# A kernel of Fourier mixing and a gated feed-forward layer on one core: the order of the first loads

## The chip, the core and the metric

The kernel runs on one core of one Trainium2 chip. The metric is device time in microseconds (us) of one execution; the lower the better. TensorE does the matrix products, VectorE and ScalarE prepare their operands and take the results out, GpSimd does a little arithmetic and issues some transfers, SyncE issues most loads.

## What is computed

The reference, cut to what matters (one batch, sequence S = 2048, width D = 640, hidden F = 1536):

```python
x = A_x
xn = _layernorm(x, axis=-1)
a = einsum("bsd,ed->bse", xn, dft_hid_re)
b = einsum("bsd,ed->bse", xn, dft_hid_im)
s = einsum("ts,bse->bte", dft_seq_re, a) - einsum("ts,bse->bte", dft_seq_im, b)
g = silu((silu(xn @ w_gate) * (xn @ w_up)) @ w_down)
return x + s * g
```

The rows of x are normalised; the sequence transform (2048 x 2048, a real and an imaginary matrix) and the hidden transform (640 x 640) are applied; a gated feed-forward layer works on the same normalised rows; the two results are multiplied and added to x.

## The kernel before

All is in float32. To get its precision from products with one pass, each operand is split into a high half (the rounded value, a copy on ScalarE) and a low half (the rest, a subtraction on VectorE), and every product is done as three matmuls: high by high, high by low, low by high (`split`, `mm3`). The large products follow a Strassen scheme, so that sums of blocks are operands too.

The work comes in stages: the sequence transform in four passes (`seq(0)` to `seq(3)`), the hidden transform (`hid_s`), then gate and up and down for two halves of the sequence (`gate_up`, `down`). All operations are first recorded in a plan with a due time, `Plan.schedule` gives each a planned start, `Plan.place` gives the buffers their places in on-chip memory from those times, and then all are written out in the order of their planned starts. Each engine runs its own instructions in that order. In the first pass (k == 0) the planned starts are fixed by hand (`pl.fixed`). The trace names the helper at line 82 (`Engine.__getattr__`, through which every operation goes) for all of them, so instructions are told apart by their tiles.

The opening of the first pass is written in `opening()`, with tables of times in us: OPEN_DMA is the order of the first loads, OPEN_LN the times of the layer norm of the row tiles, OPEN_T those of the splits of the row tiles, OPEN_S those of the splits of the sequence matrices. A row tile is 128 rows of x with all 640 columns (320 KB, tile xn, from in_x). An operand is 128 x 1024 elements of the real or imaginary sequence matrix (512 KB, tile raw, from in_cs); it serves two row tiles, 512 columns each. In OPEN_DMA an entry (k,) is row tile k, and an entry (i, g) is the operand of pair g, real for i = 0 and imaginary for i = 1. The loop over OPEN_DMA gives the entries planned starts 0.45 us apart, and SyncE issues them in that order.

The products of the opening go over row tiles kk = 0 to 7, and for each tile first the real and then the imaginary operand (in tile 7 the other way round). Each has three products with 512 columns: two into a pair of banks and one into a third bank. Those of tile 0 are done unsplit in float32, two weight loads each; those of the others are the three matmuls of `mm3`, so nine weight loads for each operand. Tile 0 is normalised in an own, shorter way. For the others VectorE takes the statistics (bn_stats, bn_aggr), ScalarE the root, VectorE the reciprocals, ScalarE normalises the tile in place and copies its high half, VectorE makes the low half. Eleven matmuls on a tile of zeros (`busy`) run on TensorE before the first product.

```python
t = -6.0
for what in OPEN_DMA:
    if len(what) == 1:
        load_x(what[0], at(t), nc.sync)
    else:
        fetch(what[0], what[1], t, *what[2:])
    t += 0.45
```

Of the kernel before, what the change touches and what calls it, by code (L numbers as in the profile page):

```python
# [278 lines left out]
def tile_fnet_swiglu(  # L279
# [448 lines left out]


    OPEN_DMA = ((0,), (0, 0), (1,), (1, 0), (2,), (3,), (0, 1), (1, 1), (4,), (5,), (0, 2), (1, 2), (6,), (7,), (0, 3), (1, 3))  # L730
    OPEN_LN = ((0, 1, (-2.5,), (-1.4, -1.0, -0.5), (0.4,)),
               (1, 1, (0.5,), (1.6, 1.9), (2.8,)),
               (2, 1, (3.5,), (5.0, 5.3), (6.1,)),
# [8 lines left out]
    def seq(k):  # L742
# [112 lines left out]
        def opening():  # L855
# [566 lines left out]
```

## Time and profile before

| what | value |
|---|---|
| median of 3 runs | 969.66 us (969.62 to 969.9) |
| the profiled execution, its own time | 969.83 us |
| its span, first to last instruction | 967.6 us |
| TensorE busy | 961.7 us, 99% of the span |
| VectorE busy | 734.6 us, 76% |
| ScalarE busy | 488.6 us, 50% |
| GpSimd busy | 121.3 us, 13% |
| mean granted clock of TensorE | 0.999 |

The profile is of one execution, by the hardware profiler. PE is TensorE's matmuls, PEld its weight loads (which overlap the matmuls), DVE is VectorE, ACT ScalarE, POOL GpSimd, SP SyncE; a q behind the name is the engine's sequencer, which issues transfers. A row of the timeline has start, length, engine, line, operation, output<-inputs, shapes, count, and in brackets the idle time of the engine ahead of it with what ended it. A tile is named without its number: hl is a split operand, raw an unsplit one, xn the row tiles, sm, mv, bst and rowst the small results of the layer norm, ps the banks of the products. KB are 1024 bytes in the DMA views; MB and GB/s are decimal.

### The profile page before, as it was taken

What the parts mean: (1) busy time and instruction counts of PE and PEld (TensorE: products, weight loads), DVE (VectorE), ACT (ScalarE), POOL (GpSimd) and SP (SyncE); (2) the same over time, 40 slices, a digit from 0 to 9 for tenths busy, and PEclk for the clock granted to TensorE, in tenths of its full rate; (3) what the DMA queues carried; (4) which work ended last, traced back from release to release, by engine and by line L of the source; (5) the groups of instructions that cost most, each with busy time, mean ns of one, the idle gap of its engine ahead of it and who ended that gap; (6) DMA issues with size and microseconds to landing.
All of it is one profiled execution on the core that took longest, in us unless ns stands there. A gap on an engine that the chain in (4) does not pass through costs nothing.

```text
span 967.6 us, 11521 instructions
## 1 busy us (share of the span) xinstructions
PE 961.7 (99%) x4235; PEld 792.0 (82%) x4235; DVE 734.6 (76%) x932; ACT 488.6 (50%) x676; POOL 121.3 (13%) x184
## 2 busy tenths in 40 slices
PE   9999999999999999999999999999999999999998
PEld 5888888888888888888888888888888888888887
DVE  7889668757774687676987898999978666666775
ACT  5686445454545455544356555563446444444341
POOL 1460211011101110111100211210002000000000
PEclk9999999999999999999999999999999999999999
DMA  9997848494938497778673374439699330105793
GB/s 352 283 249 215 233 147 229 152 271 106 231 109 255 109 236 263 208 196 253 170 213 131 141 265 155 168 136 289 222 292 256 99 133 4 55 1 163 240 346 131
DMA packets 64056, 186.50 MB, mean 193 GB/s; under 512 B 6528, under 2 KB 10368, under 8 KB 64000
## 3 DMA queue, kind: packets, MB, share of 16 engines
q1 hardware_dynamic: 45952, 125.45, 39.0%
q0 software_dynamic: 18048, 60.32, 24.2%
q8 instruction: 33, 0.54, 0.2%
q14 instruction: 23, 0.19, 0.1%
HBM read 151.39 MB, written 34.36 MB: 192 GB/s over the span
## 4 chain that ended last, share of the span: by engine, by line
PE 99%; DMA 0%; DVE 0%; ACT 0%; issue 0%; DVEq 0%; ACTq 0%
PE ps L82 99%; DMA xn<-in_x 0%; DVE raw L82 0%; DVE bst L82 0%; DVE sm L82 0%; ACT raw L82 0%; ACT sm L82 0%; DVE mv L82 0%; DVEq L82 0%; ACTq L82 0%
## 5 line engine op out<-in xcount | busy, mean ns | idle before, releaser
L82 PE MATMUL ps<-hl 128*128 128x512 f32 (+1 forms) x3258 | 780.1, 388 | 0.0
L82 PEld LDWEIGHTS ps<-hl 128*128 128x128 f32 x3258 | 610.1, 188 | 126.6 <-DVE hl L82 0.6
L82 DVE TENSOR_TENSOR hl<-raw,hl 128x1024 fp32r<-128x1024 f32 (+5 forms) x360 | 346.5, 994 | 134.3 <-ACT hl L82 94.4
L82 ACT ACTIVATE hl<-raw 128x1024 fp32r<-128x1024 f32 (+6 forms) x416 | 325.0, 826 | 170.3 <-DVE raw L82 84.8
L82 PE MATMUL ps<-hl,hl 128*128 128x512 f32 (+1 forms) x954 | 259.9, 388 | 0.0
L82 ACT ACTIVATE raw<-ps 128x512 f32<-128x512 f32 (+1 forms) x144 | 97.9, 681 | 231.4 <-PE ps L82 225.2
L82 PEld LDWEIGHTS ps<-hl,hl 128*128 128x128 f32 x954 | 179.0, 188 | 36.9
L82 DVE TENSOR_TENSOR raw<-raw 128x1024 f32<-128x1024 f32 (+7 forms) x216 | 178.6, 849 | 19.8 <-ACT raw L82 15.5
L82 DVE TENSOR_TENSOR raw<-ps,raw 128x512 f32<-128x512 f32 (+1 forms) x95 | 77.2, 814 | 48.4 <-PE ps L82 47.6
L82 DVE TENSOR_TENSOR raw<-raw,raw 128x512 f32<-128x512 f32 (+3 forms) x50 | 44.2, 892 | 6.5 <-ACT raw L82 4.3
L82 ACT ACTIVATE hl<-xn 128x1024 fp32r<-128x1024 f32 (+3 forms) x61 | 42.2, 723 | 13.6 <-PE ps L82 9.1
L82 POOL DMA_DIRECT2D p_dram<-raw x24 | 16.4, 686 | 251.4 <-DVE raw L82 215.7
L82 ACT ACTIVATE raw<-raw 128x512 f32<-128x512 f32 (+1 forms) x30 | 21.5, 718 | 46.7 <-DVE raw L82 46.7
L82 DVE TENSOR_TENSOR hl<-xn,hl 128x1024 fp32r<-128x1024 f32 (+3 forms) x50 | 40.8, 833 | 4.0 <-PE ps L82 3.9
L82 POOL DMA_DIRECT2D raw<-in_cs x36 | 32.5, 984 | 57.7 <-DMA raw<-in_cs 29.1
L82 DVE SCALAR_TENSOR_TENSOR hl<-raw,hl 128x256 fp32r<-128x256 f32 (+4 forms) x56 | 32.7, 586 | 4.0 <-ACT hl L82 4.0
L82 POOL DMA_DIRECT2D out<-raw x10 | 6.9, 689 | 226.6 <-DVE raw L82 197.3
L82 POOL DMA_DIRECT2D d_p<-hl x28 | 15.2, 543 | 71.4 <-ACT hl L82 59.6
L82 ACT ACTIVATE xn<-xn,sm,rowst 128x640 f32<-128x640 f32 (+1 forms) x16 | 14.1, 906 | 5.3 <-DVE sm L82 3.6
L82 DVE BATCH_NORM_STATS2 bst<-xn 128x6 f32<-128x320 f32 x32 | 13.7, 479 | 4.0 <-DMA xn<-in_x 4.0
L82 POOL DMA_DIRECT2D y_dram<-raw x12 | 8.2, 683 | 64.6 <-DVE raw L82 46.2
L82 POOL DMA_DIRECT2D raw<-p_dram x8 | 10.1, 1267 | 44.7 <-DVE raw L82 26.3
(42 smaller groups left out, 84.3 us busy)
## 6 DMA issues: line engine op xcount, KB each, us to landing
raw<-in_cs SPq DMA_DIRECT2D x84, 512.0 KB, 7.0
hl<-d_p SPq DMA_DIRECT2D x56, 384.0 KB, 5.0
raw<-in_cs POOLq DMA_DIRECT2D x36, 512.0 KB, 9.8
raw<-in_wb SPq DMA_DIRECT2D x24, 640.0 KB, 4.7
d_p<-hl POOLq DMA_DIRECT2D x28, 384.0 KB, 4.0
p_dram<-raw POOLq DMA_DIRECT2D x16, 512.0 KB, 4.4
raw<-p_dram SPq DMA_DIRECT2D x8, 768.0 KB, 8.5
xn<-in_x SPq DMA_DIRECT2D x16, 320.0 KB, 9.8
```

What stands on the lines that cost most here:

```text
L82: return real(*args, **kw)
```

## The change

Two pairs of neighbours in OPEN_DMA change places: the first imaginary operand is loaded ahead of row tile 1, and the second real operand ahead of row tile 3. Nothing else is edited.

```diff
-    OPEN_DMA = ((0,), (0, 0), (1,), (1, 0), (2,), (3,), (0, 1), (1, 1), (4,), (5,), (0, 2), (1, 2), (6,), (7,), (0, 3), (1, 3))
+    OPEN_DMA = ((0,), (0, 0), (1, 0), (1,), (2,), (0, 1), (3,), (1, 1), (4,), (5,), (0, 2), (1, 2), (6,), (7,), (0, 3), (1, 3))
```

## Rows read from the trace of the kernel before

**Rows 1.** The page, part 4: shares of the chain by engine.

```profile
PE 99%; DMA 0%; DVE 0%; ACT 0%; issue 0%; DVEq 0%; ACTq 0%
```

**Rows 2.** The chain in order of time: start, length, what.

```profile
0.73 3.01 DMA xn<-in_x
...
6.46 956.86 PE ps L82 x4224
```

**Rows 3.** Groups of weight loads, 17 to 962.5 us: busy, mean | idle before, releasers.

```profile
L82 PEld LDWEIGHTS ps<-hl 128*128 128x128 f32 x3234 | 605.8, 188 | 124.9
L82 PEld LDWEIGHTS ps<-hl,hl 128*128 128x128 f32 x952 | 178.6, 188 | 36.9
```

**Rows 4.** Timeline of SyncE's queue, 0 to 7 us.

```profile
1.16 0.42 SPq L82 DMA_DIRECT2D raw<-in_cs  x1
1.63 0.42 SPq L82 DMA_DIRECT2D xn<-in_x  x1
2.10 0.43 SPq L82 DMA_DIRECT2D raw<-in_cs  x1
...
6.87 0.33 SPq L82 DMA_DIRECT2D raw<-in_cs  x1
```

**Rows 5.** DMA issues: the ones at 1.16 and 1.63 us, us to landing last.

```profile
raw<-in_cs SPq DMA_DIRECT2D x1, 512.0 KB, 4.1
...
xn<-in_x SPq DMA_DIRECT2D x1, 320.0 KB, 5.2
```

**Rows 6.** Windows between landings: length, engines busy, PEclk, DMA share, GB/s.

```profile
5.24:6.86 1.62, 1.34 (x4) 0.33 (x3) 1.31 (x7) 0.65 (x2) 0.00 (x0) 1.00 1.04 268
6.86:9.21 2.35, 2.35 (x6) 0.76 (x4) 1.82 (x8) 1.11 (x2) 0.19 (x1) 1.00 0.91 304
10.98:12.23 1.25, 1.25 (x5) 0.64 (x4) 1.10 (x6) 0.78 (x3) 0.25 (x1) 1.00 1.01 408
```

**Rows 7.** Timeline of the weight loads, 6.4 to 17 us.

```profile
8.28 0.19 PEld L82 LDWEIGHTS ps<-raw,xn 128*128 128x128 f32 x1 [0.24 <-issue]
9.25 0.30 PEld L82 LDWEIGHTS ps<-raw 128*128 128x128 f32 x2 [0.78 <-DMA raw<-in_cs]
...
11.50 0.19 PEld L82 LDWEIGHTS ps<-hl 128*128 128x128 f32 x1 [0.24 <-issue]
11.93 4.09 PEld L82 LDWEIGHTS ps<-hl 128*128 128x128 f32 x18 [0.24 <-DVE hl L82]
16.42 0.76 PEld L82 LDWEIGHTS ps<-hl 128*128 128x128 f32 x4 [0.40 <-DVE hl L82]
```

**Rows 8.** Timeline of VectorE, 7 to 18.5 us.

```profile
7.09 0.88 DVE L82 BATCH_NORM_STATS2 bst<-xn 128x6 f32<-128x320 f32 x2
...
10.25 0.89 DVE L82 BATCH_NORM_STATS2 bst<-xn 128x6 f32<-128x320 f32 x2 [0.20 <-DMA xn<-in_x]
...
13.20 0.88 DVE L82 BATCH_NORM_STATS2 bst<-xn 128x6 f32<-128x320 f32 x2
...
14.61 0.42 DVE L82 SCALAR_TENSOR_TENSOR hl<-xn,hl 128x256 fp32r<-128x256 f32 x1 [0.28 <-ACT hl L82]
...
15.15 1.22 DVE L82 TENSOR_TENSOR hl<-raw,hl 128x1024 fp32r<-128x1024 f32 x1
```

**Rows 9.** Timeline of ScalarE, 8 to 18 us.

```profile
9.49 0.92 ACT L82 ACTIVATE xn<-xn,sm,rowst 128x640 f32<-128x640 f32 x1 [0.95 <-DVE sm L82]
10.44 0.61 ACT L82 ACTIVATE hl<-xn 128x256 fp32r<-128x256 f32 x2
...
12.25 1.06 ACT L82 ACTIVATE hl<-raw 128x1024 fp32r<-128x1024 f32 x1 [0.49 <-DMA raw<-in_cs]
```

**Rows 10.** Windows at the end, columns as in rows 6.

```profile
963.31:965.00 1.69, 0.00 (x0) 0.00 (x0) 0.85 (x2) 0.38 (x1) 0.00 (x0) 1.00 0.40 155
965.00:966.00 1.00, 0.00 (x0) 0.00 (x0) 0.00 (x0) 0.00 (x0) 0.00 (x0) 0.71 0.37 131
```

## The prediction

> **Names.** x0, x1, x2, x3 are the first row tiles (320 KB each). R0, R1 are the first two real operands and I0, I1 the imaginary ones; each is 512 KB and serves a pair of row tiles (R0 and I0 serve x0 and x1, R1 and I1 serve x2 and x3). Step k is the products of row tile k, first the real three, then the imaginary three. Before: x0 R0 x1 I0 x2 x3 R1 I1. After: x0 R0 I0 x1 x2 R1 x3 I1.
>
> **What bounds the kernel now.** I read the chain that ended last first: 99% of the span is TensorE [rows 1], and in order of time the chain is 3.01 us of waiting for x0, 2.7 us of layer norm, and from 6.46 us on TensorE without a break for 956.86 us [rows 2]. Then the weight loads: from 17 us to the end of the products not one of them waits for another engine [rows 3]. Two things follow. What is lost or gained before 17 us moves the end by the same amount, since no later wait can swallow it. And nothing behind the opening has anything left to give.
>
> In the opening TensorE stops twice after its start [rows 7]. The load at 9.25 us waits for I0. The loads before it came every 0.43 us, so 8.71 was due; a load that starts a pause over is followed by the next after 0.11 us and not 0.43, so the pause costs 9.25 + 0.11 - 9.14 = 0.22 us. The load at 16.42 is the second of step 2. It waits for VectorE, which makes the low half of R1 from 15.15 to 16.37 [rows 8]; by the pace of 0.23 us (18 loads in 4.09 us) it was due at 16.07 and the next at 16.30; the next came 0.11 behind it, at 16.53, so this pause costs 0.23 us.
>
> Who sets 16.37? VectorE. From 7.09 on it runs in its written order: statistics of x1, its root, low half of R0, statistics of x2, low halves of x1, and so on, with a few tenths idle [rows 8]. x1 landed at 6.83 (issued at 1.63, 5.2 us later [rows 4, 5]; SyncE's issue at 6.87 is released by it) and VectorE took it 0.26 us later, at once after x0's work. So row tile 1 has almost no slack now.
>
> **The change, part by part.** No engine's instruction is added or removed: four entries of the list OPEN_DMA change places in pairs, each with a planned start 0.45 us away from the old one. All operations of the first real pass carry fixed planned times, so VectorE, ScalarE, GpSimd and TensorE keep their order, and only SyncE's order changes. The 0.42 us that an issue takes, row tile or operand [rows 4], is the same in any order.
>
> *I0 earlier.* It is put ahead of 320 KB that took 1.62 us between two landings [rows 6] but 0.8 to 1.1 us by its bytes at the 408 and 304 GB/s of the stretches behind (328 thousand bytes each; I take 0.9). It lands at some 9.21 - 0.9 = 8.3 us, before 8.71. The pause of 0.22 us at step 0's imaginary half goes; step 1 could then start at 11.71 instead of 11.93.
>
> *x1 later.* The transfers of one queue land in the order of issue, so x1 now lands when the bytes of x0, R0, x1 and I0 are all there. That is the moment at which I0 landed before: 9.21 us (the release of the load at 9.25 [rows 7]). So x1 moves from 6.83 to 9.21, and its statistics from 7.09 to 9.23: +2.14 us. Bounds: if I0 moved at the 1.25 us that R1 took between its neighbour's landing and its own [rows 6], x1 would land at 6.83 + 1.25 = 8.08 (+1.01). If x1 still had some 0.4 us to go on the slowest engine behind I0, it would land at 9.6 (+2.5). I take 9.21, since it is the same bytes in the same early stretch, which ran at 268 and 304 GB/s and not at 408 [rows 6].
>
> The Trainium skill (DMA: Bandwidth & Descriptors, section Specifications) gives a ceiling of 435 GB/s for the core's DMA engines, by which I0 would delay x1 by an estimated 1.21 us; the later stretch at 408 GB/s agrees, the early one does not. By that page the sum below would be 970.3 us.
>
> *From x1's delay to TensorE.* Behind x1 VectorE runs its chain with the same lengths, +2.14. The 0.20 us that it now idles for x2 at 10.25 are used up, but this helps only the low halves of x1: the root of x2 comes from ScalarE, whose work on x1 is 2.14 late as well. ScalarE waits 0.49 us for R1 at 12.25 [rows 9]. After the change R1 is there by then (below), so ScalarE is late by about 1.65 from there. VectorE idles 0.28 us for ScalarE at 14.61 [rows 8]; counted from the earliest start that the 0.09 us overlap of neighbouring rows allows (14.24) this is 0.37 us, and it is swallowed. So the low half of x2 moves by 2.14 - 0.37 = 1.77 (to 16.38), and the low half of R1 ends at 18.14 instead of 16.37.
>
> TensorE: step 1 needs x1's high half. It now ends at 11.05 (9.49 + 0.92 for the normalised rows, then 0.61 for two copies [rows 9]); the first and larger copy, which is all that the load needs, ends some 0.2 us sooner, at 10.86, and will at 13.0. So step 1 starts at 13.15 instead of 11.71: 1.44 us idle. Its third load, due at 13.40, needs the low half, which ends at 13.54: 0.18 more, of which 0.05 are left after the restart. Eighteen products at 0.23 bring step 2 to 17.4; its second load comes at 18.18 instead of 16.42. **TensorE is 1.76 us later there.** As a ledger: idle 1.44 + 0.05 + 0.03 + 0.67 = 2.19 new, less 0.22 + 0.23 of today's pauses, gives 1.74; the two agree. Behind it VectorE is late by 1.77 and TensorE by 1.76, so their distance is today's, and today it is enough at every load [rows 3].
>
> *R1 ahead of x3.* R1 would land about 0.8 us earlier (12.23 to 11.4), x3 at R1's old 12.23. x3 is first used at 13.20 [rows 8], 15.3 after the change: nothing waits for it. R1's use at 12.25 is moved to 13.8 by x1: its earlier landing is worth nothing beyond the 0.49 us above. Alone, without x1's delay, this half would free the 0.23 us pause at 16.42. So this part counts for 0 here, and 0.23 us gain if x1 were in time.
>
> *The queue.* SyncE's ninth and later issues each wait for the landing of the one eight before, as 6.87 shows [rows 4]. The eleventh will wait for I0 (8.3 instead of 6.87) and the twelfth for x1 (9.2, as now for I0). Six transfers are in flight in front of them then, so their data is late by nothing.
>
> **Sum.** The profiled execution took 969.83 us, of which 967.6 are the span; +1.76 gives a span of 969.4 and 971.6. The median of the three runs is 969.66, 0.17 below it, so against the median: 969.66 + 1.76 = **971.4 us**, +0.18%. A change of 0.2% is 1.94 us, about what a measurement of this kernel can tell from no change; the forecast stands just inside it.
>
> **Rivals.**
> 1. *I0 is quick in its new place.* The early stretch is slow for another reason than I0's bytes, and x1 comes only 1.25 to 1.8 us later (lands 8.1 to 8.65). Then the delay is the landing less 7.44: 0.64 to 1.2 us, 970.3 to 970.9. For it: R0, of the same size, landed at 5.26 (issued 1.16, 4.1 later [rows 4, 5]), 1.5 us behind x0 at 3.74 [rows 2]. Against it: x1 itself moved at only 268 GB/s in 5.24 to 6.86 [rows 6].
> 2. *The pause lowers TensorE's clock.* TensorE stands still for 1.44 us from 11.7 on, longer than anywhere between its first and last product now. If the granted clock falls from 2.4 to 1.2 GHz behind it, the 18 products of step 1 take up to 8.2 instead of 4.1 us [rows 7]; step 2's second load then comes as late as 21.4 instead of 18.18, and with part of that the total is +3 to +5 us: 973 to 974.6. For it: at the tail the last product ends at 963.3, and the granted clock is still 1.00 until 965 and 0.71 in the next microsecond [rows 10]: it does fall soon after a stop. Against it: that stop is longer, and full speed held through the shorter pauses. The Trainium skill (TensorE: Matmul & The Clock Gate, Part 1) says that the throttled state is the default and activity releases it; the fall at the tail agrees, and no row here shows a pause of this length.
> 3. *Not slower.* Both landings overlap on the 16 DMA engines so far that x1 lands by 7.44. Up to there the slack at 14.61 swallows its delay and the time stays at 969.7; with x1 quite in time both pauses, 0.22 and 0.23, would go: 969.2 us. It decides at 7.44 us, 0.6 behind today's landing. Against it: the 524 thousand bytes of I0 in 0.6 us would be 870 GB/s, and the fastest stretch of [rows 6] has 408.
> 4. *The change does not do only what it says.* The planned starts of I0 and R1 move by 0.45 us, and these enter the placement of buffers; another placement would bring other waits anywhere, a few tenths to 3 us either way. Against it: the order in which these buffers come up stays the same, and their neighbours in time too.
>
> **How the numbers follow.** Forecast (x1 between 8.65 and 9.6, +1.2 to +2.2): 0.70, with about a quarter of it above +1.94. Rival 1: 0.15. Rival 2: 0.10. Rival 3: 0.02. Rival 4: 0.03. The range takes the forecast's own, 970.9 to 971.9, and most of rival 1, and reaches a little over the upper bound: 970.3 to 972.2. Slower by over 0.2%: 0.18 + 0.10 + 0.02 = 0.30; faster: 0.02; within: 0.68.
>
> **What the profile after would show.** x1's statistics start at about 9.23; the loads of step 0's imaginary half run on at 8.71 without a wait; the first load of step 1 comes near 13.05 released by ScalarE; the second of step 2 near 18.2 released by VectorE; no wait behind 19 us; granted clock 1.00 throughout. A statistics start under 8.7 means rival 1; a granted clock under 1.00 between 11 and 20 us means rival 2. A wait of weight loads after 20 us would make the sum wrong.

## The result, and the profile after

| what | before | after |
|---|---|---|
| median (14 runs each) | 969.78 us | 971.52 us |
| lowest to highest | 969.54 to 969.96 | 971.14 to 972.70 |
| the profiled execution, its own time | 969.83 us | 971.50 us |
| its span | 967.6 us | 969.3 us |

The change makes the kernel slower: by 1.74 us or 0.18% between the medians, with a ratio of 1.0020 and a 95% interval of 1.0013 to 1.0028. Forecast were 971.4 us (+0.18%) within 970.3 to 972.2. The median sits just inside the bound of 0.2%, as forecast, and the ratio on it.

The first view is the chain that ended last, in order of time (start, length, what). Before, it began with the transfer of x0 [rows 2]:

```profile
2.11 7.00 DMA xn<-in_x
...
9.13 0.90 DVE bst L82 x2
...
11.54 0.93 ACT xn L82
```

It now begins with the transfer of x1, issued at 2.11 us and landed at 9.11, and goes through the statistics, the root and the normalising of row tile 1. x0 is no longer on it. The timeline of VectorE shows the same wait and what follows from it:

```profile
9.13 0.89 DVE L82 BATCH_NORM_STATS2 bst<-xn 128x6 f32<-128x320 f32 x2 [2.24 <-DMA xn<-in_x]
...
12.02 0.88 DVE L82 BATCH_NORM_STATS2 bst<-xn 128x6 f32<-128x320 f32 x2
...
16.30 0.37 DVE L82 SCALAR_TENSOR_TENSOR hl<-xn,hl 128x256 fp32r<-128x256 f32 x1
...
16.79 1.22 DVE L82 TENSOR_TENSOR hl<-raw,hl 128x1024 fp32r<-128x1024 f32 x1
```

VectorE stands still for 2.24 us until x1 is there; its statistics start 2.04 us later than in [rows 8] (7.09). The wait for x2 and the idle 0.28 us ahead of the low half of x2, both in [rows 8], are used up, and the low half of R1 starts at 16.79 instead of 15.15: of 2.04 us, 1.64 arrive there.

The weight loads of TensorE (to be held against [rows 7]):

```profile
8.68 0.19 PEld L82 LDWEIGHTS ps<-raw 128*128 128x128 f32 x1 [0.24 <-issue]
...
10.82 0.19 PEld L82 LDWEIGHTS ps<-raw,xn 128*128 128x128 f32 x1 [0.24 <-issue]
12.96 0.30 PEld L82 LDWEIGHTS ps<-hl 128*128 128x128 f32 x2 [1.95 <-ACT hl L82]
13.49 1.68 PEld L82 LDWEIGHTS ps<-hl 128*128 128x128 f32 x8 [0.23 <-DVE hl L82]
15.39 1.90 PEld L82 LDWEIGHTS ps<-hl 128*128 128x128 f32 x9 [0.22 <-DVE hl L82]
18.06 0.77 PEld L82 LDWEIGHTS ps<-hl 128*128 128x128 f32 x4 [0.77 <-DVE hl L82]
```

The gain that the change makes is there: the load at 8.68 (step 0's imaginary half) runs on without the wait for I0 that stood at 9.25. Then TensorE has nothing: the first load of step 1 comes at 12.96, released by ScalarE's high half of x1, and the second of step 2 at 18.06 instead of 16.42. That is 1.64 us, and the span is 1.7 us longer. Behind it no load waits, as before [rows 3]; the groups of weight loads from 19 to 964 us name no releaser here either:

```profile
L82 PEld LDWEIGHTS ps<-hl 128*128 128x128 f32 x3232 | 605.5, 188 | 124.9
L82 PEld LDWEIGHTS ps<-hl,hl 128*128 128x128 f32 x952 | 178.6, 188 | 36.8
```

ScalarE takes R1 without the wait of 0.49 us in [rows 9]:

```profile
13.54 0.28 ACT L82 ACTIVATE sm<-mv,sm 128x1 f32<-128x1 f32 x1
13.72 1.04 ACT L82 ACTIVATE hl<-raw 128x1024 fp32r<-128x1024 f32 x1
```

The clock did not move. Windows of the pause of step 1, of the steps behind it and of the rest (columns as in [rows 6]; PEclk is the third number from the end):

```profile
11.25:13.10 1.85, 0.73 (x3) 0.14 (x2) 1.78 (x7) 1.53 (x4) 0.00 (x0) 1.00 1.02 410
13.10:20.00 6.90, 6.55 (x27) 4.80 (x28) 6.29 (x20) 5.58 (x11) 0.51 (x2) 1.00 1.03 419
20.00:962.00 942.00, 942.00 (x4166) 780.58 (x4165) 719.82 (x888) 476.74 (x656) 119.31 (x172) 1.00 0.63 190
```

### The profile page after: what moved, and what is told of

Same layout as the page of the kernel before. It is cut to its first block, busy times and chain, and to the rows that moved or that the text cites. A ratio compares the mean times of both kernels' runs of the same rounds, so it can differ in the third digit from the quotient of the medians.

```text
span 969.3 us, 11521 instructions
## 1 busy us (share of the span) xinstructions
PE 962.2 (99%) x4235; PEld 792.1 (82%) x4235; DVE 734.4 (76%) x932; ACT 488.3 (50%) x676; POOL 121.0 (12%) x184
## 4 chain that ended last, share of the span: by engine, by line
PE 98%; DMA 1%; DVE 1%; ACT 0%; SPq 0%; issue 0%; DVEq 0%
PE ps L82 98%; DMA xn<-in_x 1%; DVE hl L82 0%; DVE bst L82 0%; SPq L82 0%; DVE sm L82 0%; ACT xn L82 0%; DVE raw L82 0%; ACT hl L82 0%; ACT sm L82 0%; DVE mv L82 0%; ACT raw L82 0%; DVE rowst L82 0%; DVEq L82 0%
## 5 line engine op out<-in xcount | busy, mean ns | idle before, releaser
L82 POOL DMA_DIRECT2D raw<-in_xt x6 | 6.9, 1294 | 70.6 <-DVE raw L82 70.6
```

The lines of the kernel that those rows point to most:

```text
L82: return real(*args, **kw)
```

## The experiments

The theory: the whole loss is the landing of x1, and from 7.44 us on each microsecond of it is one of the time. x0 to x3, R0, R1, I0 and I1 are as in the prediction. A single execution differs from the next by a few tenths of a microsecond, so the profiled execution is read beside its own time, and the medians (11 runs where not said otherwise) stand with their ratio to before.

**Only the first swap (e1_i0_only).**

```diff
-    OPEN_DMA = ((0,), (0, 0), (1,), (1, 0), (2,), (3,), (0, 1), (1, 1), (4,), (5,), (0, 2), (1, 2), (6,), (7,), (0, 3), (1, 3))
+    OPEN_DMA = ((0,), (0, 0), (1, 0), (1,), (2,), (3,), (0, 1), (1, 1), (4,), (5,), (0, 2), (1, 2), (6,), (7,), (0, 3), (1, 3))
```

> Only the first swap: I0 ahead of x1, with x3 ahead of R1 as before. Theory (the whole loss is x1's later landing, carried by VectorE's chain): x1 lands at 9.1 us again, R1 at about 12 and so ahead of ScalarE's use at 13.7; the second load of step 2 comes near 18.1 and the time is that of both swaps, 971.5 us. Rival (the swap of R1 and x3 takes or gives a share of its own): the time differs from 971.5 by 0.2 us or more, and some wait between 12 and 18 us is another one.

Measured: 971.51 us, ratio 1.0019 (1.0010 to 1.0028); before 969.77. The weight loads of its profile:

```profile
12.79 0.30 PEld L82 LDWEIGHTS ps<-hl 128*128 128x128 f32 x2 [1.70 <-ACT hl L82]
...
17.89 0.76 PEld L82 LDWEIGHTS ps<-hl 128*128 128x128 f32 x4 [0.77 <-DVE hl L82]
```

They are those of both swaps, 0.17 us sooner, and x1 landed 0.16 sooner too (8.95). I0 ahead of x1 is the whole loss; the swap of R1 and x3 adds nothing to it and takes nothing off.

**Only the second swap (e2_r1_only, and the same kernel profiled again, e10_r1_again).**

```diff
-    OPEN_DMA = ((0,), (0, 0), (1,), (1, 0), (2,), (3,), (0, 1), (1, 1), (4,), (5,), (0, 2), (1, 2), (6,), (7,), (0, 3), (1, 3))
+    OPEN_DMA = ((0,), (0, 0), (1,), (1, 0), (2,), (0, 1), (3,), (1, 1), (4,), (5,), (0, 2), (1, 2), (6,), (7,), (0, 3), (1, 3))
```

> Only the second swap: R1 ahead of x3, with x1 ahead of I0 as before. Theory: x1 is in time (lands near 6.8), ScalarE no longer waits for R1 at 12.25, the pause of 0.23 us at the second load of step 2 goes and the pause for I0 at step 0 stays: 969.5 us, 0.2 less than before. Rival (x3 is what is late next, or VectorE is held by something else): the pause stays, 969.7 us or more.

> A second look at e2_r1_only, in which I0 landed at 9.78 and not at 9.21 as before, and TensorE waited for it. If R1 right behind I0 delays it as a rule, I0 lands behind 9.5 again and the time is 969.9 or more; if that landing was chance, it is near 9.2, the pauses are 0.2 us and none at step 2, and the time is near 969.5.

Measured: 969.90 us, ratio 1.0001 (0.9992 to 1.0010); the second profile 969.91 in one run. The weight loads of the first profile, then of the second, up to 17.5 us:

```profile
9.82 0.30 PEld L82 LDWEIGHTS ps<-raw 128*128 128x128 f32 x2 [1.68 <-DMA raw<-in_cs]
...
12.51 5.00 PEld L82 LDWEIGHTS ps<-hl 128*128 128x128 f32 x22 [0.24 <-DVE sm L82]
```

```profile
9.60 0.30 PEld L82 LDWEIGHTS ps<-raw 128*128 128x128 f32 x2 [1.09 <-DMA raw<-in_cs]
...
12.28 5.21 PEld L82 LDWEIGHTS ps<-hl 128*128 128x128 f32 x23 [0.24 <-DVE sm L82]
```

The pause at step 2 did go: 22 and 23 loads in a row, across the place where one waited at 16.42. But nothing came of it, since TensorE now waits longer for I0, which landed at 9.78 and 9.56 and not at 9.21. The time is that of the rival, for another reason than the rival's: the pause it wanted to stay is gone. The pause at step 2 had been a reserve. Three profiles have R1 ahead of x3, and x1 ahead of the whole of I0 in the queue. In them I0 landed 0.35 us (e10_r1_again), 0.57 (e2_r1_only) and 0.80 (e7_r1_in_slot, below) later than before, and the products ended only 0.06, 0.29 and 0.53 us later. So before, I0 could have landed some 0.23 us later at no cost, though no run tries that in the old order. That R1 close behind I0 delays it fits both profiles and isn't shown by them.

**Half of I0 ahead of x1 (e3_half_i0).** Its first half serves step 0, its second step 1.

```diff
-    OPEN_DMA = ((0,), (0, 0), (1,), (1, 0), (2,), (3,), (0, 1), (1, 1), (4,), (5,), (0, 2), (1, 2), (6,), (7,), (0, 3), (1, 3))
+    OPEN_DMA = ((0,), (0, 0), (1, 0, 0), (1,), (1, 0, 1), (2,), (0, 1), (3,), (1, 1), (4,), (5,), (0, 2), (1, 2), (6,), (7,), (0, 3), (1, 3))
```

> Both swaps, but I0 is loaded as two halves of 256 KB: the half of row tile 0 ahead of x1, the half of row tile 1 behind it. A dose of half. Theory (loss = landing of x1 less 7.44): x1 lands at 7.5 to 8.0, the loss is 0.1 to 0.6 us, 969.8 to 970.3; no pause for I0 at step 0. Rival (it is the number or order of transfers, or TensorE's pause as such, and not x1's landing): 971 us or more.

Measured: 971.36 us, ratio 1.0016 (1.0007 to 1.0025); the profiled execution took 970.63. By the median the rival holds, by the profile the theory does, for VectorE's and TensorE's timelines show an opening as fast as before:

```profile
7.45 0.89 DVE L82 BATCH_NORM_STATS2 bst<-xn 128x6 f32<-128x320 f32 x2 [0.21 <-DMA xn<-in_x]
...
16.37 1.23 PEld L82 LDWEIGHTS ps<-hl 128*128 128x128 f32 x6 [0.36 <-DVE hl L82]
```

x1 landed at 7.43, and step 2's second load came at 16.37, 0.05 earlier than before. The products ended at 963.26 us against 963.30. Yet the span is 968.4, not 967.6: from the last product to the end it took 5.15 us, before 4.31. The next two kernels take this apart. The profiled execution is the fastest of the 11: the median lies 1.59 us above that of before, and the 0.75 us of it that the end does not explain are in no profile.

**One transfer more, and nothing else (e8_seventeenth).** The last operand of the opening is loaded as two halves.

```diff
-    OPEN_DMA = ((0,), (0, 0), (1,), (1, 0), (2,), (3,), (0, 1), (1, 1), (4,), (5,), (0, 2), (1, 2), (6,), (7,), (0, 3), (1, 3))
+    OPEN_DMA = ((0,), (0, 0), (1,), (1, 0), (2,), (3,), (0, 1), (1, 1), (4,), (5,), (0, 2), (1, 2), (6,), (7,), (0, 3), (1, 3, 0), (1, 3, 1))
```

> The order of before, with the last operand of the opening (imaginary, fourth pair) loaded as two halves, so SyncE issues one transfer more. Theory: the opening is as before and the products end at the same time; at the end SyncE's waits for its eight semaphores stand in a fixed order, the last output now signals the first of them instead of the last, and the seven waits behind it come after the landing: 970.6 us, 0.84 more, all of it behind the last product. Rival (the order of the waits costs nothing): 969.8 us, and the stretch behind the last product stays at 4.31 us.

Measured: 970.69 us, ratio 1.0010 (1.0002 to 1.0019), 0.99 more than before (969.70) and near the 970.6 of the theory. What SyncE waited for at the end of the span, first before, then here:

```profile
SPq L1418 <- DMA out<-raw: 0.7, 1, 0.7
```

```profile
SPq L1418 <- DMA out<-raw: 1.5, 1, 1.5
```

The products ended at 963.17, no later than before, and the rest took 5.13 us instead of 4.31. SyncE's transfers signal eight semaphores (counters that tell of a landing) in turn, and at the end of the program SyncE waits for the eight in a fixed order. Before, the last output signals the last of them, and no other wait for a landing stands behind it. With one transfer more it signals the first: released at 966.49, the seven others follow one by one until 967.32. So 0.82 us belong to the number of transfers, and to nothing in the opening.

The same profile shows what set step 2's second load in the old order:

```profile
16.29 1.23 PEld L82 LDWEIGHTS ps<-hl 128*128 128x128 f32 x6 [0.32 <-DVE hl L82]
```

R1 landed at 12.10 instead of 12.23, and the load came 0.13 us earlier than at 16.42: it follows R1 there.

**Half of I0 ahead of x1, transfers as many as before (e9_half_16).** The order of e3_half_i0, with the entry (7,) left out and row tiles 6 and 7 in one transfer.

```diff
-                if len(what) == 1:
+                if what == (6,):
+                    load_x2(6, at(t), nc.sync)
+                elif len(what) == 1:
...
+    def load_x2(k, lead, eng):
+        pl.prod(lead, lambda: eng.dma_start(
+            xn_tiles(k, 2), x[k * P:(k + 2) * P, :].rearrange("(k p) d -> p k d", p=P)), [], [(xn, k), (xn, k + 1)])
```

> As e3_half_i0 (half of I0 ahead of x1, half behind it, R1 ahead of x3), but row tiles 6 and 7 are one transfer, so that SyncE's transfers are as many as before. Theory: the 0.84 us between the last product and the end of the span that e3_half_i0 had more than before go, and what is left is the landing of x1 less 7.44 (0 to 0.75 us): 969.8 to 970.5 us. Rival (the 0.84 us come from the halves, or from the opening): the time stays within 0.3 us of e3_half_i0, 971.1 or more.

Measured: 970.51 us, ratio 1.0010 (1.0001 to 1.0019), 0.85 less than e3_half_i0, or 0.78 with each against its own before (969.70 here, 969.77 there). It is at the upper end of the theory, and the rival falls: the stretch behind the last product is back at 4.33 us.

```profile
7.88 0.89 DVE L82 BATCH_NORM_STATS2 bst<-xn 128x6 f32<-128x320 f32 x2 [0.71 <-DMA xn<-in_x]
...
16.81 0.77 PEld L82 LDWEIGHTS ps<-hl 128*128 128x128 f32 x4 [0.75 <-DVE hl L82]
```

**x2 ahead of x1 as well (e4_x2_first).**

```diff
-    OPEN_DMA = ((0,), (0, 0), (1,), (1, 0), (2,), (3,), (0, 1), (1, 1), (4,), (5,), (0, 2), (1, 2), (6,), (7,), (0, 3), (1, 3))
+    OPEN_DMA = ((0,), (0, 0), (1, 0), (2,), (1,), (0, 1), (3,), (1, 1), (4,), (5,), (0, 2), (1, 2), (6,), (7,), (0, 3), (1, 3))
```

> Both swaps, and x2 ahead of x1 besides. A dose of one and a third. Theory: x1 lands 0.75 us later than with both swaps, near 9.9, and everything behind it is later by as much: loss 2.4, 972.2 us, with TensorE's pause ahead of step 1 some 2.1 us long. Rival 1 (slack swallows a part): under 972.0. Rival 2 (a longer pause lowers TensorE's granted clock): under 1.00 between 11 and 20 us and 973.5 us or more.

Measured: 972.81 us (5 runs), ratio 1.0032 (1.0020 to 1.0045). x1 landed at 10.47, later than expected, since I0 did too (8.71, with both swaps 7.81). Loads, then the clock in the pause and behind it:

```profile
14.32 0.30 PEld L82 LDWEIGHTS ps<-hl 128*128 128x128 f32 x2 [3.21 <-ACT hl L82]
...
19.43 0.53 PEld L82 LDWEIGHTS ps<-hl 128*128 128x128 f32 x3 [0.77 <-DVE hl L82]
```

```profile
11.35:14.40 3.05, 0.67 (x3) 0.07 (x1) 2.45 (x10) 1.75 (x5) 0.19 (x1) 1.00 1.03 416
14.40:20.00 5.60, 5.25 (x21) 3.75 (x22) 5.00 (x17) 4.52 (x9) 0.51 (x2) 1.00 1.03 417
```

TensorE stood still for 2.38 us of the first window (3.05 less 0.67 busy; with both swaps it was 1.85 less 0.73, so 1.12), and the granted clock stayed at 1.00. Both rivals fall.

**The doses together.** For each profiled execution: when x1's statistics start, that start less 7.46 (the landing less 7.44), how much later than 16.42 step 2's second load comes, and how much the execution took over the 969.83 us of before.

| kernel | statistics | by the rule | second load | time |
|---|---|---|---|---|
| e3_half_i0 | 7.45 | -0.01 | -0.05 | +0.80 (0.84 of it at the end) |
| e9_half_16 | 7.88 | +0.42 | +0.39 | +0.45 |
| e1_i0_only | 8.97 | +1.51 | +1.47 | +1.49 |
| both swaps | 9.13 | +1.67 | +1.64 | +1.67 |
| e4_x2_first | 10.50 | +3.04 | +3.01 | +2.98 |

From 7.4 to 10.5 us the loss follows x1's landing one for one, and the line meets the time of before at 7.44 within some 0.1 us. Before itself lies off the line (statistics at 7.09, no loss), so it does bend; no kernel of the table has x1 between 6.86 and 7.42 (e7_r1_in_slot below has it at 7.34, but TensorE waits for I0 there), so where it bends, and that the time is flat up to there, is read from the line and not measured.

**x1 out of the queue (e6_x1_act).** Both swaps, with x1 issued by ScalarE.

```diff
-                    load_x(what[0], at(t), nc.sync)
+                    load_x(what[0], at(t), nc.scalar if what[0] == 1 else nc.sync)
```

> Both swaps, but x1 is issued by ScalarE (right behind its first small instruction, near 2.2 us) and not by SyncE: it no longer stands behind I0 in one queue. Theory (the loss is x1's place behind I0): x1 shares the DMA engines with R0 and I0 and lands near 6.5, I0 lands before 8.7, both pauses go: 969.3 to 969.6 us (SyncE's transfers are one fewer, which may add 0.1 at the end). Rival 1 (x1 now takes its bytes from R0): R0 lands behind 6.4 and TensorE starts later, 970 us or more. Rival 2 (the engines still serve x1 behind I0): x1 near 9, 971.5 us.

Measured: 969.96 us, ratio 1.0001 (0.9992 to 1.0010). The loss is gone: x1, issued at 1.33 us and not near 2.2, landed at 6.73, its statistics start at 7.03, and no load waits at step 1 or 2. But it is not a gain either. ScalarE, VectorE and TensorE:

```profile
1.33 0.38 ACTq L82 DMA_DIRECT2D xn<-in_x  x1
...
6.58 0.63 ACT L82 ACTIVATE hl<-raw 128x512 fp32r<-128x512 f32 x1 [1.35 <-DMA raw<-in_cs]
```

```profile
7.03 0.88 DVE L82 BATCH_NORM_STATS2 bst<-xn 128x6 f32<-128x320 f32 x2
```

```profile
9.36 0.38 PEld L82 LDWEIGHTS ps<-raw 128*128 128x128 f32 x2 [0.48 <-DMA raw<-in_cs]
...
12.12 5.43 PEld L82 LDWEIGHTS ps<-hl 128*128 128x128 f32 x24 [0.24 <-DVE sm L82]
```

x1 is served beside R0 and I0, and both land later: with both swaps R0 landed at 5.44 and I0 at 7.81, here at 6.56 and 9.32. So the theory is right on x1 and the loss, and wrong on I0 (before 8.7) and on the time (969.3 to 969.6). Rival 1 came true in kind (R0 behind 6.4) and nearly in price: step 1's run of loads starts at 12.12, 0.19 us later than before (11.93 in [rows 7]). The pause at step 2 is gone, and the products end 0.11 us earlier than before; the stretch behind them took 4.44 us, 0.13 more, with the last output landing 3.50 us behind the last product instead of 3.28. Rival 2 falls.

**I0's first half behind x1, with R1 ahead of x3 (e5_split_behind).** A try at a kernel better than both: x0 R0 x1, then I0 as two halves, x2, R1, x3, I1; row tiles 6 and 7 in one transfer.

```diff
-    OPEN_DMA = ((0,), (0, 0), (1,), (1, 0), (2,), (3,), (0, 1), (1, 1), (4,), (5,), (0, 2), (1, 2), (6,), (7,), (0, 3), (1, 3))
+    OPEN_DMA = ((0,), (0, 0), (1,), (1, 0, 0), (1, 0, 1), (2,), (0, 1), (3,), (1, 1), (4,), (5,), (0, 2), (1, 2), (6,), (0, 3), (1, 3))
```

> x1 stays ahead of I0, I0 is loaded as two halves of 256 KB (the half of row tile 0 first), R1 goes ahead of x3, and row tiles 6 and 7 are one transfer, so that SyncE's transfers are as many as before. Theory: x1 lands near 6.8 as before, the first half of I0 before 8.7, so the pause for I0 at step 0 goes; the pause at step 2 goes too, since ScalarE no longer waits for R1: 969.3 us, 0.45 under before. Rival (something else is late next, such as the second half of I0 or x2): a wait of the weight loads between 9 and 17 us stays and the time is 969.6 or more.

Measured: 970.10 us, ratio 1.0003 (0.9994 to 1.0012). The first half alone landed at 9.44, later than the whole of I0 before (9.21):

```profile
9.48 0.30 PEld L82 LDWEIGHTS ps<-raw 128*128 128x128 f32 x2 [1.11 <-DMA raw<-in_cs]
...
16.60 0.99 PEld L82 LDWEIGHTS ps<-hl 128*128 128x128 f32 x5 [0.37 <-DVE hl L82]
```

The rival holds: the pause at step 0 stays, and one at step 2 as well, since x2 landed at 10.84 and not at 10.23 as before and VectorE waited 0.91 us for it. In e3_half_i0 and e9_half_16 the same half, one place further ahead, landed at 6.57 and 6.75; behind x1 it needed 3 us for 256 KB.

**What makes the early transfers slow (e7_r1_in_slot).**

```diff
-    OPEN_DMA = ((0,), (0, 0), (1,), (1, 0), (2,), (3,), (0, 1), (1, 1), (4,), (5,), (0, 2), (1, 2), (6,), (7,), (0, 3), (1, 3))
+    OPEN_DMA = ((0,), (0, 0), (1,), (0, 1), (1, 0), (2,), (3,), (1, 1), (4,), (5,), (0, 2), (1, 2), (6,), (7,), (0, 3), (1, 3))
```

> x0 R0 x1 R1 I0: R1 in the place that I0 has before, and I0 behind it; x2, x3 and I1 follow. It asks what makes I0's transfer slow (mean packet 267 ns before and 261 with both swaps, 159 for the operands behind). If it is the early stretch, R1's packets take about 260 ns here and I0's 159, and I0 lands near 10.2. If it is I0's own data, R1's take about 159 and I0's 260, and I0 lands near 10.4. The time tells little: I0 lands 1.0 to 1.3 us later than before, and TensorE waits for it, 970.5 to 971.0 us.

Measured: 970.40 us (8 runs), ratio 1.0007 (0.9997 to 1.0018), just under what was expected. TensorE waits for I0, which landed at 10.01:

```profile
10.05 0.30 PEld L82 LDWEIGHTS ps<-raw 128*128 128x128 f32 x2 [1.64 <-DMA raw<-in_cs]
```

By the packets of the trace (128 of 4096 bytes for an operand) R1's took 182 ns on the mean in that place and I0's 189 behind it. Neither theory holds: R1 is slower there than elsewhere (159), far from I0's 260, and I0 is faster than in its own place but not at 159. What slows the first 9 us stays open.

## Why the prediction was right

**x1's landing.** Forecast 9.21 (same bytes, same early stretch), measured 9.11 and in e1_i0_only 8.95. The low end, 8.08 by the later stretch's pace, would have given 970.3. But the early stretch kept its slow pace in the new order too; this is the window from R0's landing to I0's, columns as in [rows 6]:

```profile
5.44:7.81 2.37, 2.37 (x5) 0.89 (x4) 1.34 (x7) 1.44 (x2) 0.00 (x0) 1.00 0.88 256
```

Rival 1 falls with it. The Trainium skill (DMA: Bandwidth & Descriptors, section Specifications) states a ceiling of 435 GB/s; the stretches of 410 to 419 GB/s above come near it, and the 256 GB/s here stay far below. The premise that the loads of one queue land in the order of issue held: in all twelve profiles SyncE's loads did. That the sum came within 0.1 us is better than its terms were and in part luck: the last of the same four transfers x0, R0, x1, I0 landed between 8.95 and 9.78 in the six profiles that load them first and whole from one queue, and I0 (7.81, forecast 8.3) and x1 behind it (1.30 us, forecast 0.9) missed in opposite directions.

**From the landing to TensorE.** Forecast: the delay less 0.37, 1.76 us at step 2's second load; measured 1.64, from statistics 0.10 earlier than forecast. The table of doses bears out the prediction's rule for rival 1, landing less 7.44. (x1's landing before is 6.86 by [rows 6] and not 6.83; the sum goes by the statistics and doesn't change.) Single terms were off by little: the second load of step 1's imaginary half waited 0.18 us (15.39, due 15.21) where 0.03 was reckoned, and the pause ahead of step 1 cost 1.39 (from 11.68 to 13.07) where 1.44 was.

**The gain at step 0.** It came (no wait at 8.68; I0 landed at 7.81, forecast 8.3) and was worth nothing, as forecast, because step 1 waits for x1 anyway.

**R1 ahead of x3.** Counted 0: e1_i0_only shows it (971.51 without it, 971.52 with it). The sentence beside it failed: that alone it would free 0.23 us. The pause went and the time stayed (969.90 and 969.91, before 969.77), because I0 is late next. The step left out was to ask whether I0's landing is fixed when the transfers behind it change; the two profiles had it 0.57 and 0.35 us later.

**Rival 2, the clock.** Shown wrong for pauses of this length: 1.12 us without a product with both swaps and 2.38 in e4_x2_first left it at 1.00. The tail, which spoke for this rival, is not the same in each execution: before, the clock fell within 2.7 us of the last product [rows 10], and after, where the last product ended at 964.98, it had not fallen 4.2 us later:

```profile
967.00:969.20 2.20, 0.00 (x0) 0.00 (x0) 0.00 (x0) 0.00 (x0) 0.00 (x0) 1.00 0.19 63
```

No run here shows from which length on a pause costs the clock.

**Rival 3, not slower.** x1 landed 1.67 us behind its bound of 7.44. That bound fits the line of the doses; the flat stretch below it was not measured. Its 969.2 us was reached by no kernel's median, as the whole of I0 never landed by 8.7 with x1 in time.

**Rival 4, other placements.** On TensorE, VectorE, ScalarE and GpSimd the order of work is the same in both profiles, and no wait of weight loads beyond 19 us appeared.

**The spread.** Before, x1 had some 0.25 us of slack for VectorE and 0.35 more for TensorE. After, its landing sets the time, and the runs spread over 1.56 us instead of 0.42. In the other sets of runs, though, those of before spread over 0.48 to 1.13 us. That the wider spread is that of the landing is argued from the doses; single landings of runs without a profile aren't seen.

## What to carry to other kernels

When two loads change places, work out both landings from the bytes ahead of each, and then ask for each load how long its consumer could still wait: here the first load that was moved up had a pause of 0.22 us to win, none of which could be used behind the next wait, and the one moved back had 0.6 us of slack against a delay of 2.25. Here the small load whose data start a long chain across three engines had to stay ahead of the large one that feeds products directly. A pause that a reordering removes may have been the reserve of the next wait, so look for what is late next before counting it as gain.

## What the runs showed that was not expected

- One transfer more in the opening costs 0.82 us at the other end of the program, since SyncE's last waits stand in a fixed order and the number of its transfers decides which of them the last output releases (4.31 us behind the last product against 5.13 and 5.15). An experiment that splits a load has to keep their number.
- Half the bytes hardly landed sooner: 256 KB behind x1 landed at 9.44, the whole 512 KB in the same place at 9.21 and 9.18 (before and e8_seventeenth), and with R1 ahead of x3, as with the half, at 9.56 and 9.78. In the first 9 us a landing is not read off the bytes alone.
- TensorE's granted clock stayed full through 2.38 us without a product, and in the profile after through the 4.2 us behind the last one.
